# Lightning attention and a gated FFN on one core: q ahead of k in the block loads, a wait ahead of block 0's stores, four iotas in place of two and two adds

## The chip, the cores and the metric

The kernel runs on one core of a Trainium2 chip. A core has five engines with their own instruction queues: TensorE (PE in the profile, and PEld for its weight loads), VectorE (DVE), ScalarE (ACT), GpSimd (POOL) and SyncE (SP, which here only issues transfers). They meet through semaphores. Transfers are carried out by 16 DMA engines that all queues share. The metric is the device time of one execution in microseconds (us). Before the change it is 227.37 us, the median of 8 runs between 227.23 and 227.91.

## What is computed

Inputs are q, k, v of shape (4 batches, 8 heads, 768 positions, 64), one decay factor per head, and three FFN weight matrices (512 x 1536 twice, 1536 x 512). The first half is causal linear attention with decay, defined over blocks of 64 positions with a running state per batch and head; the second half is a feed-forward layer with a sigmoid gate on the 3072 tokens.

```
for b in range(nb):                       # blocks of 64 positions
    intra = einsum(qb, kb) * Dmask        # Dmask[i, j] = lam ** (i - j) for i >= j, else 0
    intra = einsum(intra, vb)
    inter = einsum(qb * lam_pow, kv_state)
    out[block] = intra + inter
    kv_state = lam ** 64 * kv_state + einsum(kb * rev_pow, vb)
...
gate = 1 / (1 + exp(-(x @ w_gate)))
out = (gate * (x @ w_val)) @ w_out        # fp32, 3072 x 512
```

## The kernel before

The 768 positions are cut into six steps n = 0 to 5 of 128 positions (the text calls them blocks 0 to 5), each with all four batches: 512 tokens. For every block PE does three things: the attention of the block; the two products with w_gate and w_val (`gp` and `vp` in `piece_gv`, L488), in 12 slices `ft` of 128 columns; and the product with w_out (`po`, L522), one per batch. While PE does the FFN of block n, the pieces of the attention of block n+1 are put between its slices. The order of every engine's instructions is the order in which the program emits them; no scheduler changes it. The list `more[ft]` in the main loop holds the pieces that are emitted after slice ft.

For a block from 2 on, the attention of that block uses these steps, named by function:

- `load` (L94 and L100): three transfers per q or k and one for v, issued on GpSimd's queue, from fp32 in HBM to bf16 in SBUF, in pieces of 64 numbers.
- `xbar` (L298): SyncE issues two transposing transfers, `kt<-kb` and `qt<-qb`, from SBUF to SBUF.
- `gate` (L615): GpSimd copies one column of each transposed tile to a scratch tile. Since GpSimd works in order, what it issues afterwards, v of the same block and k and q of the next, starts only when both transposes have landed. `next_loads(n)` emits `xbar(n)`, `gate(n)`, the load of v of n, and the loads of n+1.
- `e_q` (L277): VectorE multiplies the transposed q by a table of powers, giving QS, one instruction for two batches.
- `chunk_s` (L387, `sp`): PE multiplies QS with the transposed k, `kt`. `chunk_m` (L397): VectorE masks it.
- `piece_kd` (L127): ScalarE scales k, in four pieces of two heads, giving `kd`.
- `chunk_c` (L447, `cp`): PE multiplies `kd` with v, which yields the update of the state. `decayed` (L456, `xd`) is the old state times its decay on VectorE; `update_0` (L464) and `update_1` (L472) add the two.

In the loop for n = 1, which works ahead for block 2, `next_loads(2)` is emitted after slice 2, and right behind it, after slice 3, the eight stores of block 0's result, of 128 KB each. All of them are issued by SyncE, so its queue reads: the two transposes of block 2, eight stores of block 0, the two transposes of block 3 (emitted after slice 8), four stores of block 1, and so on. At the start of the program GpSimd issues the first loads between small table instructions; two of these are iotas that write a column each of `jn` (L174), the exponents of a block of 128, and two VectorE instructions in `chunk_rows` (L218, L219) turn them into exponents for half blocks of 64. `jn` is read by ScalarE in `tables_late`.

The lines in the main loop that set the places before the change are these:

```
more[2 + late + bp].append(do(e_q, nx, [2 * bp, 2 * bp + 1]))
more[4 + late].append(do(chunk_s, nx, bp))
more[8].append(do(chunk_c, nx, bp, cs))
more[6 + late].append(do(decayed, nx))
more[3 + late + i].append(kd(nx, 2 * i))
more[2].append(lambda: next_loads(2))
```

Here `nx` is n + 1 and `late` is 1 for n = 1 and 0 otherwise.

Of the kernel before, what the change touches and what calls it, by code (L numbers as in the profile page):

```python
# [16 lines left out]
def kernel(  # L17
# [11 lines left out]
    nc = tc.nc  # L29

    B, H, S, D = q.shape
    C = 128
# [28 lines left out]
    L = C // 2  # L61
    SYNC = mybir.DependencyInfo(mybir.DependencyClass.Sync, mybir.DependencyReason.DATA)
# [19 lines left out]
    def rows_of(u):  # L82
        return slice(u * 64, (u + 1) * 64)

    def load(n, what, b0=0, b1=B):
        sl = slice(n * C, (n + 1) * C)
        for c in what:
            if (c, n) not in T_:
                T_[c, n] = qkv.tile([128, B, H, D], BF16, tag=c + "b", name=c + "b",
                                      bufs=5 if c == "v" else 4)  # L90
            src = {"q": q, "k": k, "v": v}[c]
            nat = b1 if n == 0 or c == "v" else min(b1, NB2)
            if b0 < nat:
                nc.gpsimd.dma_start(  # L94
                    out=T_[c, n][:, b0:nat],
                    in_=src[b0:nat, :, sl, :].rearrange("b h s d -> s (b h) d"))
            if nat < b1:
                m = max(nat, b0)
                for u in range(2):
                    nc.gpsimd.dma_start(  # L100
                        out=T_[c, n][:, m:b1, u::2, :],
                        in_=src[m:b1, 1 - u::2, sl, :].rearrange("b h s d -> s (b h) d"))
# [29 lines left out]
    jn = const.tile([128, 2], FP32, tag="jn")  # L132
# [31 lines left out]
    for u in range(2):  # L164
# [4 lines left out]
                            pattern=[[1, C]], channel_multiplier=-1)  # L169
    nc.gpsimd.iota(ip1, pattern=[[1, C]], base=1, channel_multiplier=0,  # L170
                   allow_small_or_imprecise_dtypes=True)
    load(0, "k", 2, 4)
    for i, base in enumerate((-1, C - 1)):
        nc.gpsimd.iota(jn[:, i:i + 1], pattern=[[0, 1]], base=base, channel_multiplier=-1,  # L174
                       allow_small_or_imprecise_dtypes=True)
    nc.gpsimd.affine_select(out=tri, in_=tri, compare_op=ALU.is_gt, fill=1.0, base=0,
                            pattern=[[-1, C]], channel_multiplier=1)
# [35 lines left out]

    def powers(u):
        nc.scalar.activation(mask0[:, u], mask0[:, u], AF.Exp)

    def chunk_rows():
        nc.vector.tensor_scalar_add(jn[rows_of(1), 0:1], jn[rows_of(1), 0:1], float(L))  # L218
        nc.vector.tensor_scalar_add(jn[rows_of(0), 1:2], jn[rows_of(0), 1:2], -float(L))  # L219

    def tables_late():
        nc.scalar.activation(pk[:, 1], lnl, AF.Exp, scale=jn[:, 0:1])
# [37 lines left out]
    QT, KT = {}, {}  # L260
    tqs, tks = {}, {}

    def t_(c, n, bs, pool=ps_at, tag="ps"):
        ps = pool.tile([128, len(bs), HP, C], BF16, name="t" + c, tag=tag)
        for i, b in enumerate(bs):
            for hp in range(HP):
                nc.tensor.transpose(ps[:, i, hp, :], T_[c, n][:, b, 2 * hp:2 * hp + 2, :], ident)
        (tqs if c == "q" else tks)[n, bs[0]] = ps
# [24 lines left out]
        nc.vector.tensor_copy(T_[c, 0][:, b], H32[c, b])  # L293

    def xbar(n):
        for c, d in (("k", KT), ("q", QT)):
            d[n] = qtp.tile([128, B, HP, C], BF16, tag=c + "t", name=c + "t")
            nc.sync.dma_start_transpose(  # L298
                out=d[n].rearrange("p b hp s -> p (b hp) s"),
                in_=T_[c, n].rearrange("p b h d -> p (b h d)"))  # L300
        for b in range(B):
            KS[n, b] = KT[n][:, b]
# [172 lines left out]

    HT = {}

    def piece_gv(n, ft):  # L480
        fs = slice(ft * 128, (ft + 1) * 128)
        gp, vp = (ps_ff.tile([128, 2, TCH // 2], FP32, name=c, tag="ff") for c in ("gp", "vp"))
        sg = htp.tile([128, TCH], BF16, tag="sg", name="sg", bufs=3)
        whole, first, second = slice(0, 2), slice(0, 1), slice(1, 2)

        def product(ps, W, part):
            for mt in range(NMT):
                nc.tensor.matmul(ps[:, part], lhsT=W[:, mt, fs], rhs=XT[n][:, part, mt],  # L488
                                 start=(part is not second and mt == 0),
                                 stop=(part is not first and mt == NMT - 1), skip_group_check=True)  # L490

        order = [(gp, WG, whole), (vp, WV, whole)]
        if ft == 0 and n == 0:
            order = [(gp, WG, first), (gp, WG, second), (vp, WV, whole)]
        elif ft == 0 and n == 1:
            order = [(gp, WG, first), (vp, WV, first), (gp, WG, second), (vp, WV, second)]
        for ps, W, part in order:
            product(ps, W, part)
            if ps is gp and part is not first:
                nc.scalar.activation(sg, gp.rearrange("p a b -> p (a b)"), AF.Sigmoid)  # L500
        HT[n, ft] = htp.tile([128, TCH], BF16, tag="ht", name="ht", bufs=2 * NFT)
        if n < FIRST_XBAR:
            nc.vector.tensor_mul(HT[n, ft], sg, vp.rearrange("p a b -> p (a b)"))  # L503
        else:
            nc.vector.tensor_mul(HT[n, ft].rearrange("p (b c i) -> p c b i", b=B, c=2),  # L505
                                 sg.rearrange("p (c b i) -> p c b i", c=2, b=B),
                                 vp.rearrange("p c (b i) -> p c b i", b=B))

    OB, PO = {}, {}

    def store(n, tt, c0=0, c1=DM):
        (nc.scalar if (n, tt, c1) == (NSTEP - 1, B - 1, DM) else nc.sync).dma_start(out=out[tt * S + n * C:tt * S + (n + 1) * C, c0:c1],
                          in_=OB[n, tt][:, c0:c1])

    def piece_po(n, tt, c0, c1, eng, fts):
# [5 lines left out]
        for ft in fts:  # L521
            nc.tensor.matmul(po[:, :c1 - c0], lhsT=HT[n, ft][:, tt * 128:(tt + 1) * 128],  # L522
                             rhs=WO[:, ft, c0:c1], start=(ft == 0), stop=(ft == NFT - 1))
# [21 lines left out]
    cast_hw("k", 1)  # L545
    zeros(3)
    powers(1)
    chunk_rows()
    t_("q", 0, [0])
    e_q(0, [0], nc.vector)  # L550
    t_("q", 0, [1])
# [54 lines left out]
    load(1, "q", 2, 4)  # L606
    load(1, "v", 0, 2)
    load(1, "v", 2, 4)
    load(2, "kq")

    gates = const.tile([128, 2], BF16, tag="gates")

    def gate(n):
        for i, t in enumerate((KT[n], QT[n])):
            nc.gpsimd.tensor_copy(gates[:, i:i + 1], t[:, B - 1, HP - 1, C - 1:C])  # L615

    def next_loads(n):
        xbar(n)
        gate(n)
        load(n, "v")  # L620
        if n + 1 < NSTEP:
            load(n + 1, "kq")

# [5 lines left out]
    def gv(n, ft, *more):  # L631
        unit(lambda: piece_gv(n, ft), *more)

    def po(n, tt, *more, c=(0, DM), eng=nc.scalar, fts=range(NFT)):
        unit(lambda: piece_po(n, tt, *c, eng, fts), *more)
# [16 lines left out]
    def do(f, *args, **kw):  # L652
        return lambda: f(*args, **kw)
# [24 lines left out]
    def kd(n, h0, h1=None, **kw):  # L678
        return do(piece_kd, n, range(h0, h1 or h0 + 2), **kw)
# [20 lines left out]
    for n in range(1, NSTEP):  # L700
        nx = n + 1
        more = [[] for i in range(NFT)]
        if nx < NSTEP:
            late = 1 if n == 1 else 0
            cs = (0, 1) if nx < NSTEP - 1 else (0,)
            for bp in range(2):
                more[2 + late + bp].append(do(e_q, nx, [2 * bp, 2 * bp + 1]))
                more[4 + late].append(do(chunk_s, nx, bp))
                more[8].append(do(chunk_c, nx, bp, cs))
            for bp in range(2):  # L710
                more[4 + late + bp].append(do(chunk_m, nx, bp))
                more[8].append(do(update_0, nx, bp))
                if 1 in cs:
                    more[9 + bp].append(do(update_1, nx, bp))
            more[6 + late].append(do(decayed, nx))
            more[3 + late].insert(0, do(make_kd, nx))
            for i in range(4):
                more[3 + late + i].append(kd(nx, 2 * i))
            more[11].append(att(nx))
        if n == 1:  # L720
            more[0].append(chunk_lamq)
            more[2].append(lambda: next_loads(2))
            more[3].extend([lambda tt=tt, j=j: store(0, tt, 256 * j, 256 * j + 256)
                            for tt in range(B) for j in range(2)])
            more[8].append(lambda: next_loads(3))
        for ft in range(NFT):
            gv(n, ft, *more[ft])
        for tt in range(B):
            if n == NSTEP - 1 and tt == B - 1:
                po(n, tt, c=(0, 384), eng=nc.vector)  # L730
                po(n, tt, c=(384, 512))
            else:
                more = [lambda n=n: next_loads(n + 3)] if tt == B - 1 and n + 3 < NSTEP else []
                po(n, tt, *more)
# [35 lines left out]
```

## Time and profile before

| what | us |
|---|---|
| median of 8 runs | 227.37 |
| the profiled execution, its own time | 227.33 |
| its span in the profile | 225.5 |
| PE busy | 217.4 |
| DVE busy | 104.2 |
| ACT busy | 106.4 |
| POOL busy | 63.9 |
| share of the 16 DMA engines taken by GpSimd's queue (q0) | 86.9% |
| share taken by the hardware queue of SP (q1) | 20.1% |

The profile is of one execution whose time is inside the range of the runs. Its times count from the start of the span, and 1.8 us of the measured time lie around the span. PE is the busiest engine by far. A busy share is a mean over the whole span; where PE is idle, it must be read from the waits and from the order of time. The clock granted to PE is 1.00 throughout.

In the timeline, a line has the start, the length, engine and line, operation, what is written and read, and in square brackets the idle time before and what ended it. In the lists of transfers, the last number is the median time from issue to landing.

### The profile page before, as it was taken

Reading aid. Unit: us, or ns where it says so; the run is one execution under the profiler, and the core shown is the slowest. Engines: PE = TensorE matmul, PEld = TensorE weight load, DVE = VectorE, ACT = ScalarE, POOL = GpSimd, SP = SyncE. Lnnn points to the kernel's source line nnn. Section 1 sums busy time; section 2 is a strip of 40 time slices with the busy share of each in tenths; the row PEclk is TensorE's granted clock in tenths of the full one; section 3 lists DMA queues with packets and bytes.
Section 4 is the critical chain, followed back from the end, with each engine's and each line's share of the span. In section 5 each row is a group of like instructions: output and inputs, shape, how many; then the busy total and the mean of one; then the engine's idle time right before and its main releaser. Section 6 shows DMA issues by size and latency. Waiting matters only on the chain.

```text
span 225.5 us, 5209 instructions
## 1 busy us (share of the span) xinstructions
PE 217.4 (96%) x2187; PEld 106.1 (47%) x2187; DVE 104.2 (46%) x196; ACT 106.4 (47%) x232; POOL 63.9 (28%) x83
## 2 busy tenths in 40 slices
PE   7799999999997999999999999999999999999994
PEld 2454444557443544444544444544444444444443
DVE  4785553439478700478800378800378500333300
ACT  5777534494374342385342385342385342333221
POOL 7998865660085008401920030000000000000000
PEclk9999999999999999999999999999999999999999
DMA  7999999999989998997999839012100012100022
GB/s 112 151 160 184 196 202 179 172 154 141 175 201 159 141 199 104 207 167 140 85 156 185 181 60 89 3 49 93 47 3 0 0 51 94 47 0 0 4 93 94
DMA packets 106008, 25.25 MB, mean 112 GB/s; under 512 B 97152, under 2 KB 103552, under 8 KB 105984
## 3 DMA queue, kind: packets, MB, share of 16 engines
q0 software_dynamic: 82944, 13.90, 86.9%
q1 hardware_dynamic: 22752, 10.95, 20.1%
q8 instruction: 17, 0.28, 0.5%
q10 hardware_dynamic: 288, 0.07, 0.1%
q14 instruction: 7, 0.06, 0.1%
HBM read 28.32 MB, written 6.29 MB: 153 GB/s over the span
## 4 chain that ended last, share of the span: by engine, by line
PE 67%; DMA 23%; POOL 6%; issue 1%; SPq 1%; ACT 0%; POOLq 0%
PE po L522 23%; PE gp L488 20%; PE vp L488 20%; DMA WO<-in_moe_w_out_dram 6%; DMA kb<-in_k_dram 4%; DMA vb<-in_v_dram 4%; DMA WV<-in_moe_w_val_dram 4%; DMA WG<-in_moe_w_gate_dram 3%; DMA qt<-qb 2%; SPq L298 1%; POOL vb L94 1%; PE cp L447 1%; PE op L411 1%; PE op L425 1%; POOL WG L105 1%
## 5 line engine op out<-in xcount | busy, mean ns | idle before, releaser
L488 PE MATMUL gp<-XT,WG 128*128 128x512 bf16 (+1 forms) x296 | 74.2, 374 | 0.4 <-DMA WG<-in_moe_w_gate_dram 0.4
L488 PE MATMUL vp<-XT,WV 128*128 128x512 bf16 (+1 forms) x292 | 74.1, 376 | 0.0
L500 ACT ACTIVATE sg<-gp 128x512 bf16<-128x512 f32 x72 | 43.0, 597 | 64.8 <-PE gp L488 61.5
L505 DVE TENSOR_TENSOR ht<-sg,vp 128x512 bf16<-128x512 bf16 x48 | 33.0, 687 | 79.9 <-PE vp L488 79.9
L522 PE MATMUL po<-WO,ht 128*128 128x512 bf16 (+2 forms) x300 | 63.9, 371 | 0.0
L488 PEld LDWEIGHTS <-WV 128*128 128x128 bf16 x292 | 28.6, 98 | 33.4
L488 PEld LDWEIGHTS <-WG 128*128 128x128 bf16 x296 | 28.1, 98 | 32.3 <-DMA WG<-in_moe_w_gate_dram 1.1
L522 PEld LDWEIGHTS <-ht 128*128 128x128 bf16 x300 | 28.3, 98 | 31.9
L526 ACT COPY ob<-po 128x512 f32<-128x512 f32 (+1 forms) x24 | 13.7, 572 | 38.8 <-PE po L522 38.8
L127 ACT ACTIVATE kd<-kb,kds 128x128 bf16<-128x128 bf16 (+1 forms) x88 | 28.8, 400 | 0.0
L503 DVE TENSOR_TENSOR ht<-sg,vp 128x512 bf16<-128x512 bf16 x24 | 16.5, 686 | 13.2 <-PE vp L488 13.2
L615 POOL COPY gates<-kt 128x1 bf16<-128x1 bf16 x4 | 0.8, 188 | 50.6 <-DMA kt<-kb 50.6
L94 POOL DMA_DIRECT2D vb<-in_v_dram x9 | 11.9, 1334 | 2.5 <-issue 1.2
L318 DVE TENSOR_TENSOR MT<-sp,mask 128x512 bf16<-128x512 f32 x16 | 9.9, 683 | 2.9 <-PE sp L310 2.9
L437 ACT CAST XT<-op 128x512 bf16<-128x512 f32 x16 | 8.2, 599 | 5.0 <-PE op L425 5.0
L397 DVE TENSOR_TENSOR MT<-sp,mask 128x512 bf16<-128x512 f32 x16 | 10.3, 682 | 0.0
L100 POOL DMA_DIRECT2D qb<-in_q_dram x10 | 8.9, 907 | 2.5 <-DMA WO<-in_moe_w_out_dram 2.5
L100 POOL DMA_DIRECT2D kb<-in_k_dram x10 | 8.8, 893 | 2.0 <-DMA WO<-in_moe_w_out_dram 0.7
L94 POOL DMA_DIRECT2D qb<-in_q_dram x8 | 9.0, 1124 | 1.1 <-POOLq L754 0.8
L536 PE MATMUL zps<-st 128*128 128x512 bf16 x18 | 7.2, 544 | 1.5 <-DVE st L159 1.5
L94 POOL DMA_DIRECT2D kb<-in_k_dram x6 | 6.9, 1158 | 1.3 <-DMA WO<-in_moe_w_out_dram 0.8
L108 POOL DMA_DIRECT2D WV<-in_moe_w_val_dram x9 | 6.8, 764 | 1.2 <-DMA WG<-in_moe_w_gate_dram 0.8
(81 smaller groups left out, 114.6 us busy)
## 6 DMA issues: line engine op xcount, KB each, us to landing
out_dram<-ob SPq DMA_DIRECT2D x19, 256.0 KB, 2.1
vb<-in_v_dram POOLq DMA_DIRECT2D x4, 512.0 KB, 7.7
qb<-in_q_dram POOLq DMA_DIRECT2D x6, 256.0 KB, 9.9
kb<-in_k_dram POOLq DMA_DIRECT2D x6, 256.0 KB, 8.6
qb<-in_q_dram POOLq DMA_DIRECT2D x12, 128.0 KB, 9.3
WO<-in_moe_w_out_dram POOLq DMA_DIRECT2D x4, 384.0 KB, 12.2
kb<-in_k_dram POOLq DMA_DIRECT2D x10, 128.0 KB, 9.1
WG<-in_moe_w_gate_dram POOLq DMA_DIRECT2D x4, 256.0 KB, 7.5
```

The source lines that it names most:

```text
L94: nc.gpsimd.dma_start(out=T_[c, n][:, b0:nat], in_=src[b0:nat, :, sl, :].rearrange("b h s d -> s (b h) d"))
L100: nc.gpsimd.dma_start(out=T_[c, n][:, m:b1, u::2, :], in_=src[m:b1, 1 - u::2, sl, :].rearrange("b h s d -> s (b h) d"))
L127: nc.scalar.mul(KD[n][:, at, i, :], T_["k", n][:, at, i, :], kds[:, min(n // FIRST_XBAR, 1), h:h + 1])
L318: nc.vector.tensor_tensor(out=MT[n, b][:, u], in0=SP[n, b][u], in1=mask0[:, 1 - u if swapped(n, b) else u], op=ALU.mult)
L397: nc.vector.tensor_tensor(out=MT[n, bp][:, u], in0=SP[n, bp][u], in1=mask[:, u ^ bp].unsqueeze(1).to_broadcast([128, 2, HP, L]), op=ALU.mult)
L437: nc.scalar.copy(XT[n][:, c, :, bp * C:(bp + 1) * C], OP[n, c, bp].rearrange("p h j i -> p h (j i)"))
L488: nc.tensor.matmul(ps[:, part], lhsT=W[:, mt, fs], rhs=XT[n][:, part, mt], start=(part is not second and mt == 0), stop=(part is not first ...
L500: nc.scalar.activation(sg, gp.rearrange("p a b -> p (a b)"), AF.Sigmoid)
L503: nc.vector.tensor_mul(HT[n, ft], sg, vp.rearrange("p a b -> p (a b)"))
L505: nc.vector.tensor_mul(HT[n, ft].rearrange("p (b c i) -> p c b i", b=B, c=2), sg.rearrange("p (c b i) -> p c b i", c=2, b=B), vp.rearrange ...
L522: nc.tensor.matmul(po[:, :c1 - c0], lhsT=HT[n, ft][:, tt * 128:(tt + 1) * 128], rhs=WO[:, ft, c0:c1], start=(ft == 0), stop=(ft == NFT - 1))
L526: (eng.copy if eng is nc.scalar else eng.tensor_copy)(o, po[:, :c1 - c0])
```

## The change

The change has five edits.

1. For blocks 2 to 5, q is loaded and transposed ahead of k: the order is turned in `load(…, "qk")`, in `xbar` and in `gate`.
2. In the loop for n = 1 the eight stores of block 0 move from behind slice 3 to behind slice 7, and ahead of them SyncE gets an empty instruction that waits for the VectorE product of slice 7 of block 1 (`MUL[1, 7]`, the `ht` of that slice). SyncE's queue keeps its order: transposes of block 2, stores of block 0, transposes of block 3.
3. `decayed` moves from behind slice 6 (7 for n = 1) to behind slice 0 (2 for n = 1).
4. `make_kd` and the four `kd` pieces move from behind slices 3 to 6 to behind slices 4 to 7 for n = 2, 3, 4; for n = 1 they were there.
5. The two iotas over a full column of `jn` become four over half columns of 64 rows that write the half-block exponents directly, and `chunk_rows` with its two VectorE instructions goes.

PE's instructions and their order are the same as before.

```diff
     load(0, "k", 2, 4)
-    for i, base in enumerate((-1, C - 1)):
-        nc.gpsimd.iota(jn[:, i:i + 1], pattern=[[0, 1]], base=base, channel_multiplier=-1,
+    for u, i, base in ((0, 0, -1), (1, 0, -1), (0, 1, L - 1), (1, 1, L - 1)):
+        nc.gpsimd.iota(jn[rows_of(u), i:i + 1], pattern=[[0, 1]], base=base, channel_multiplier=-1,
                        allow_small_or_imprecise_dtypes=True)
...
-    def chunk_rows():
-        nc.vector.tensor_scalar_add(jn[rows_of(1), 0:1], jn[rows_of(1), 0:1], float(L))
-        nc.vector.tensor_scalar_add(jn[rows_of(0), 1:2], jn[rows_of(0), 1:2], -float(L))
...
     def xbar(n):
-        for c, d in (("k", KT), ("q", QT)):
+        for c, d in (("q", QT), ("k", KT)):
...
-            nc.vector.tensor_mul(HT[n, ft], sg, vp.rearrange("p a b -> p (a b)"))
+            mul = nc.vector.tensor_mul(HT[n, ft], sg, vp.rearrange("p a b -> p (a b)"))
...
+        MUL[n, ft] = mul.ins.name
...
-    load(2, "kq")
+    load(2, "qk")
...
     def gate(n):
-        for i, t in enumerate((KT[n], QT[n])):
+        for i, t in enumerate((QT[n], KT[n])):
...
         if n + 1 < NSTEP:
-            load(n + 1, "kq")
+            load(n + 1, "qk")
...
+            more[2 * late].append(do(decayed, nx))
             for bp in range(2):
...
-            more[6 + late].append(do(decayed, nx))
-            more[3 + late].insert(0, do(make_kd, nx))
+            more[4].insert(0, do(make_kd, nx))
             for i in range(4):
-                more[3 + late + i].append(kd(nx, 2 * i))
+                more[4 + i].append(kd(nx, 2 * i))
...
             more[2].append(lambda: next_loads(2))
-            more[3].extend([lambda tt=tt, j=j: store(0, tt, 256 * j, 256 * j + 256)
+            more[7].append(lambda: tc.add_manual_dep(nc.sync.nop().ins, MUL[1, 7], SYNC,
+                                                     reason="the loads ahead of the stores"))
+            more[7].extend([lambda tt=tt, j=j: store(0, tt, 256 * j, 256 * j + 256)
                             for tt in range(B) for j in range(2)])
```

More of the change, by code (lines that the diff above doesn't have):

```diff
@@ L474, in update_1 @@
                 in1=CP[n, bp][1][:, hp], op0=ALU.mult, op1=ALU.add)
-    HT = {}
+    HT, MUL = {}, {}
     def piece_gv(n, ft):
@@ L502, in piece_gv @@
         if n < FIRST_XBAR:
-            nc.vector.tensor_mul(HT[n, ft], sg, vp.rearrange("p a b -> p (a b)"))
+            mul = nc.vector.tensor_mul(HT[n, ft], sg, vp.rearrange("p a b -> p (a b)"))
         else:
-            nc.vector.tensor_mul(HT[n, ft].rearrange("p (b c i) -> p c b i", b=B, c=2),
+            mul = nc.vector.tensor_mul(HT[n, ft].rearrange("p (b c i) -> p c b i", b=B, c=2),
                                  sg.rearrange("p (c b i) -> p c b i", c=2, b=B),
                                  vp.rearrange("p c (b i) -> p c b i", b=B))
+        MUL[n, ft] = mul.ins.name
     OB, PO = {}, {}
@@ L547 @@
     powers(1)
-    chunk_rows()
     t_("q", 0, [0])
```

## The prediction, made before the changed kernel ran

> **What bounds the kernel now.** I read the page first: busy shares and the slices of the span.
>
> ```profile
> PE 217.4 (96%) x2187; PEld 106.1 (47%) x2187; DVE 104.2 (46%) x196; ACT 106.4 (47%) x232; POOL 63.9 (28%) x83
> PE   7799999999997999999999999999999999999994
> DMA  7999999999989998997999839012100012100022
> ```
>
> PE is the bound except in the first slices and in the thirteenth (a slice is 5.6 us), near 70 us. As the change leaves PE's work and order alone, all it can move is PE's idle time. Next, PE's waits, and PE's timeline for the attention of block 2 and, behind the first line of dots, the same steps of block 3.
>
> ```profile
> PE cp L447 <- DMA vb<-in_v_dram: 1.2, 1, 1.2
> PE sp L387 <- DVE QS L277: 0.4, 1, 0.4
> PE gp L488 <- DMA WG<-in_moe_w_gate_dram: 0.4, 2, 0.2
> ```
>
> ```profile
> 63.95 0.44 PE L387 MATMUL sp<-QS,kt 64*64 64x64 bf16 x32
> 64.84 0.45 PE L387 MATMUL sp<-QS,kt 64*64 64x64 bf16 x32 [0.45 <-DVE QS L277]
> 65.22 1.04 PE L488 MATMUL gp<-XT,WG 128*128 128x512 bf16 x4
> ...
> 71.82 0.73 PE L447 MATMUL cp<-vb,kd 64*64 64x64 bf16 x64 [1.25 <-DMA vb<-in_v_dram]
> ...
> 98.11 0.74 PE L387 MATMUL sp<-QS,kt 64*64 64x64 bf16 x64
> 98.78 1.04 PE L488 MATMUL gp<-XT,WG 128*128 128x512 bf16 x4
> ...
> 105.79 0.73 PE L447 MATMUL cp<-vb,kd 64*64 64x64 bf16 x64
> ```
>
> Undisturbed, sp takes 98.78 - 98.11 = 0.67 us; in block 2 it takes 65.22 - 63.95 = 1.27. That is 0.60 lost, because QS was late. From there to cp block 3 has four slices, 105.79 - 98.78 = 7.01, block 2 three; a slice is 1.73 (100.52 to 102.25), so cp could start at 65.22 + 7.01 - 1.73 = 70.50. It starts at 71.82: 1.32 lost to v. Together 1.92 us, the most that the change can give there. Behind it PE is saturated to the end, so what is gained at cp arrives in full.
>
> Then, why QS and v are late: the queues of SyncE and GpSimd, and the chain of waits.
>
> ```profile
> 54.67 3.21 SPq L298 DMA_TRANSPOSE kt<-kb  x1
> 57.98 2.96 SPq L298 DMA_TRANSPOSE qt<-qb  x1
> 61.00 4.01 SPq L512 DMA_DIRECT2D out_dram<-ob  x8
> 76.34 3.11 SPq L298 DMA_TRANSPOSE kt<-kb  x1
> ```
>
> ```profile
> 62.85 0.19 POOL L615 COPY gates<-qt 128x1 bf16<-128x1 bf16 x1 [1.81 <-DMA qt<-qb]
> 63.30 1.68 POOL L94 DMA_DIRECT2D vb<-in_v_dram  x1 [0.26 <-issue]
> ```
>
> ```profile
> 57.98 4.82 DMA qt<-qb
> 63.30 8.48 DMA vb<-in_v_dram
> ```
>
> v is issued only when the second transpose has landed, and takes 8.48 us to 71.78, with eight stores (1 MB) issued from 61.0 to 65.0. The lists of transfers give v's landing time in the stretches 60 to 80, 84 to 96, 106 to 118 and 131 to 145 (blocks 2 to 5):
>
> ```profile
> vb<-in_v_dram POOLq DMA_DIRECT2D x1, 512.0 KB, 8.5
> ...
> vb<-in_v_dram POOLq DMA_DIRECT2D x1, 512.0 KB, 8.0
> ...
> vb<-in_v_dram POOLq DMA_DIRECT2D x1, 512.0 KB, 7.4
> ...
> vb<-in_v_dram POOLq DMA_DIRECT2D x1, 512.0 KB, 6.9
> ```
>
> Blocks 2 and 3 have stores about them (block 1's four are issued from 82.86 to 90.5), blocks 4 and 5 none; block 5 has no further loads behind it either. What is slow is the start: the software queue moved 1013 packets from 63 to 68, 4.7 us after the issue, in block 2, but 1557 from 106 to 111, 4.2 us after the issue (106.80), in block 4. At the later full rate of 1235 per us (111 to 112) block 2 is (1557 + 0.5 x 1235 - 1013) / 1235 = 0.94 us behind.
>
> **The change part by part.** The sum starts from the profiled execution, 227.33 us with a span of 225.5; the median of the runs is 227.37, 0.04 more, which I neglect. About 0.2%, 0.45 us, can be told from no change.
>
> **q ahead of k.** Of block 2, three q loads pass three k loads on GpSimd's queue, the transposes swap on SyncE, the two gate copies (0.19 each) swap: nothing is added. As the loads have one shape, qt's transpose starts at 54.67 and lands as kt did, by 60.85; both QS (0.69 each) are then made behind slices 3 and 4 before PE arrives at 63.95. sp waits for kt instead, the second transpose, landed by 62.85: 1.1 to spare. So sp loses nothing, PE gains 0.60 and could start cp at 69.90. This alone is worth nothing in the end: v, at 71.78, would take it back.
>
> **The stores behind a wait.** The product of slice 7 ends at 69.03 + 0.68 = 69.71, and 0.60 earlier after the change: stores are issued from about 69.1 to 73.1 (4.01 for eight). Between the transposes and 70 us nothing but v, then q and k of block 3, is then on the DMA engines. First, the transposes. From the first issue to the second gate copy block 2 takes 62.85 - 54.67 = 8.18, block 4, without stores, 106.14 - 98.12 = 8.02, block 3 8.46. I take 8.02: the copy starts at 62.69, v is issued 0.45 later as before, at 63.14. Second, v itself: from 6.9 to 8.5. I take 7.4, that of block 4, which has the same q and k loads behind it and no stores. Third, the released stores may meet v's end. First store bytes come about 1 us after issue (issue 61.00; 251 packets of over 512 B from 62 to 63), so at 70.1, with v due at 70.54. Bounds: 0, and 2.3, since the one store that met loads took 4.2 instead of the median 1.9; a gain is excluded, as it is added traffic. I take 0.1, near the lower end, since four-tenths of a microsecond of overlap is left. v lands at 63.14 + 7.4 + 0.1 = 70.64; cp starts 0.04 later (71.78 to 71.82), at 70.68. PE gains 71.82 - 70.68 = 1.14. Late next is still v: PE, ready at 69.90, waits 0.78.
>
> Two rules of the Trainium skill differ from these rows. The packet counts of the software queue are 24 from 65 to 66 and 361 from 66 to 67, beside 149 and 4 of the hardware queue: when v's packets flow, the stores are nearly over. "DMA: Bandwidth & Descriptors", section "Queues, rings and completion order", says that each DMA engine takes turns between the queues for which it has packets; by that, stores could have cost v only the half microsecond in which both flowed, and the sum would be 227.33 - 0.16 - 0.5 = 226.7, an estimate, against 226.2 by the landing times. The same page, "Anatomy of one DMA — SWDGE (gpsimd) path", fits 2.0 us plus bytes over 436 GB/s, for v's 1.05 MB read 4.4 us; by that v would never be waited for and the sum is 225.4, but 6.9 is the least that any row of v here shows from block 2 on.
>
> **Behind the wait on SyncE's queue** stand the stores, block 3's transposes and block 1's stores. The stores are through the queue at 73.1, before block 3's transposes could go (76.34). Their 1 MB now shares with q and k of block 3: at 250 GB/s (their rate from 62 to 65) at most 4 us. Cover: block 3's second gate copy was at 84.80 and its sp at 98.11; GpSimd issues v of block 3 at 85.46, cp is at 105.79. Output buffers are reused by the copies of block 1's results, whose stores are issued from 82.86; block 0's would land by 79 even at 5.7 each (the slowest store row). Price 0.
>
> **decayed** (1.22 us on VectorE) goes, for block 2, behind the product of slice 2, where 1.04 is idle before the next; that one slips by some 0.1, and PE reuses its buffer a slice later. Nothing waited for xd before. 0; without cover 0.2.
>
> **kd a slice later** in blocks 3 to 5. In block 3 the last piece goes from 102.08 to 103.8 and ends at 105.06, cp is at 105.79: 0.73 to spare. 0; without cover at most a piece, 1.26, per block. The excluded gain: nothing waits for ScalarE there.
>
> **Iotas.** Two took 0.17 from start to start of what follows (4.72 to 4.89); two more add 0.17. Bounds: 0 (half a column, half the cost) and 0.6 (twice the 128x128 select, 0.30). I take 0.17 on GpSimd, 0 on the path: a 128 KB q piece issued in 0.95 lands 5.6 us later, the queue moves 2367 and 2380 packets in 6 to 8 and 8 to 10, 96% of 1235 per us, and at 20.01 GpSimd ends a wait of 0.77 for a landing. Without this cover the waits for WG at 15.89 and 19.76 (0.20 and 0.23) grow by 0.17 to 0.6, most of it absorbed in the new wait for v. VectorE's two instructions (0.15 each, 7.33 to 7.66) are followed by 0.92 of idle time: 0.
>
> **Sum:** 227.33 - 1.14 = 226.2.
>
> **The rivals.** *The stores are not what makes v slow.* Its first packet comes 2.2 us after the issue in blocks 2 and 4 alike. Then v takes 8.48 from 63.14, cp starts at 71.66: 227.2. Against it stand four blocks in the right order. *v comes in time.* With block 5's 6.9, cp starts at 70.08: 225.6; landed by 69.86, all 1.92: 225.4. Against it: other loads follow this v. *Slower: the released stores run into v.* If v still starts as slowly as before, 3395 of its 4096 packets are through at 70.0, and the stores come at 70.1 among the last 700. The mechanism decides once the end of v stretches by 0.6 (0.16 gained plus 0.45); at the 2.3 above the time is 229.5, at 0.6 227.8. *That the wait does nothing*: unlikely, as the first store waits on VectorE's count.
>
> **How the numbers follow.** My forecast, v taking 7.0 to 8.0: 0.68, with 225.8 to 226.8. v in time 0.14, stores innocent 0.11, slower 0.06, else 0.01. Range 225.5 (v at 6.9, a little sooner) to 227.2 (stores innocent); outside stay the slower case and half of the full gain. Faster 0.83, same 0.10, slower 0.07.
>
> **What would show it.** No wait of sp for QS; stores from 69 us; v's landing time near 7.4 for block 2, more packets in the first 5 us; a wait of cp of 0.5 to 1.0 us. Wrong if v takes 8.5 without stores, if cp waits for kd in blocks 3 to 5, or if waits for WG grow past 0.3.

## The result, and the profile after

The changed kernel takes 225.96 us, the median of 13 runs between 225.69 and 226.93, beside 227.4 us of the kernel before (36 runs). The ratio is 0.9941 with a 95% interval from 0.9927 to 0.9955: 1.0 to 1.7 us faster. The profiled execution took 225.69 us with a span of 223.9, beside 227.33 and 225.5: 1.6 us less. The runs of the changed kernel, here and in two later sets, lie in two groups, 18 up to 226.17 and 8 from 226.46 on; the three profiled ones are of the first, so the waits read from them are those of the quicker group.

The page of the changed kernel, busy shares and slices:

```profile
PE 216.8 (97%) x2187; PEld 106.0 (47%) x2187; DVE 103.9 (46%) x194; ACT 106.4 (47%) x232; POOL 64.8 (29%) x85
PE   7798999999999999999999999999999999999994
DMA  7999999999969999999499959012100012100022
```

The dent in PE's row near 70 us is gone. One in the fourth slice is new. All waits of PE that the profile lists for it:

```profile
PE zps L533 <- DVE st L159: 1.5, 1, 1.5
PE tq L263 <- DMA qb<-in_q_dram: 0.9, 1, 0.9
PE gp L484 <- DMA WG<-in_moe_w_gate_dram: 0.8, 2, 0.7
PE sp L306 <- ACT KS L284: 0.5, 1, 0.5
PE tk L263 <- POOL jn L174: 0.2, 1, 0.2
```

The waits of sp for QS and of cp for v have left the list; the wait for WG has grown from 0.4 to 0.8. PE's timeline in block 2's attention:

```profile
64.23 0.74 PE L383 MATMUL sp<-QS,kt 64*64 64x64 bf16 x64
64.89 1.04 PE L484 MATMUL gp<-XT,WG 128*128 128x512 bf16 x4
...
70.23 0.73 PE L443 MATMUL cp<-vb,kd 64*64 64x64 bf16 x64
```

sp takes 64.89 - 64.23 = 0.66 instead of 1.27, and cp starts at 70.23 instead of 71.82 without a wait. PE arrived at sp 0.28 later than before (63.95), because of the longer wait for WG at the start: the 1.92 lost before, less 0.28, is the 1.6 us of the span.

The queues of SyncE and GpSimd, and the transfer of v:

```profile
54.47 3.26 SPq L294 DMA_TRANSPOSE qt<-qb  x1
57.84 3.09 SPq L294 DMA_TRANSPOSE kt<-kb  x1
69.46 5.37 SPq L509 DMA_DIRECT2D out_dram<-ob  x8
75.46 5.14 SPq L294 DMA_TRANSPOSE qt<-qb  x1
82.22 3.04 SPq L294 DMA_TRANSPOSE kt<-kb  x1
```

```profile
4.72 0.99 POOL L174 IOTA jn<- 64x1 f32 x4
5.79 0.30 POOL L176 TENSOR_SCALAR_AFFINE_SELECT tri<-tri 128x128 f32<-128x128 f32 x1
...
62.57 0.19 POOL L611 COPY gates<-kt 128x1 bf16<-128x1 bf16 x1 [1.36 <-DMA kt<-kb]
63.02 1.68 POOL L94 DMA_DIRECT2D vb<-in_v_dram  x1 [0.26 <-issue]
```

```profile
vb<-in_v_dram POOLq DMA_DIRECT2D x1, 512.0 KB, 7.2
```

The stores are issued from 69.46 on, but their queue (q1) has no packet from 72 to 73 and its first 95 from 73 to 74. v is issued at 63.02 and lands 7.2 us later, at 70.2, which is where cp starts: v and PE arrive together in this execution, and v is in before the first store packet flows. v's start is quicker, as the prediction named for a sign: from 63 to 68 the software queue (q0) starts 2560 packets, where it started 1013. The iotas and what they hold up cost GpSimd 5.79 - 4.72 = 1.07 instead of 0.17.

### The profile page after: what moved, and what is told of

It reads as the page before. It is cut to its first block, busy times and chain, and to the rows that moved or that the text cites. A ratio compares the mean times of both kernels' runs of the same rounds, so it can differ in the third digit from the quotient of the medians.

```text
span 223.9 us, 5209 instructions
## 1 busy us (share of the span) xinstructions
PE 216.8 (97%) x2187; PEld 106.0 (47%) x2187; DVE 103.9 (46%) x194; ACT 106.4 (47%) x232; POOL 64.8 (29%) x85
## 4 chain that ended last, share of the span: by engine, by line
PE 91%; POOL 4%; DMA 3%; issue 1%; ACT 0%; POOLq 0%
PE po L519 28%; PE gp L484 28%; PE vp L484 27%; DMA WG<-in_moe_w_gate_dram 3%; POOL vb L94 1%; PE sp L383 1%; PE cp L443 1%; PE op L407 1%; PE op L421 1%; POOL qb L94 1%; PE cp L359 1%; PE sp L306 0%; PE op L337 0%; PE tq L263 0%; PE tk L263 0%
## 5 line engine op out<-in xcount | busy, mean ns | idle before, releaser
L611 POOL COPY gates<-qt 128x1 bf16<-128x1 bf16 x4 | 1.1, 272 | 49.6 <-DMA qt<-qb 49.6
```

## The experiments

Three questions were open after the result: which of the edits carries the gain, what makes v slow, and whether the iotas, whose cost on GpSimd was far above the forecast, cost the kernel anything. Each set of four kernels ran on one chip beside runs of the kernel before; ratios are to those. v's landing times and waits are those of one profiled execution of each kernel in each set.

**q ahead of k alone**

```diff
 (kernel before)
-        for c, d in (("k", KT), ("q", QT)):
+        for c, d in (("q", QT), ("k", KT)):
...
-    load(2, "kq")
+    load(2, "qk")
...
-        for i, t in enumerate((KT[n], QT[n])):
+        for i, t in enumerate((QT[n], KT[n])):
...
-            load(n + 1, "kq")
+            load(n + 1, "qk")
```

> The kernel before with q ahead of k alone. Theory (v is the last wait in block 2, and the stores set when it lands): sp no longer waits for QS and loses nothing, but v lands as late as before, some 8.5 us after its issue; PE waits for it 0.60 us longer at cp, about 1.85 instead of 1.25, and the time stays at 227.2 to 227.5. Rival (the 0.60 us at sp is a gain of its own): 226.8, cp 0.5 us sooner.

Measured: ratio 1.0054 (1.0028 to 1.0080), slower. sp lost nothing and v took it back, as expected, and more: v took 9.1 us instead of some 8.5, and cp waited 2.46 instead of 1.85. The rest was not expected. Its timeline of PE, and then stretches of 1 us with the granted clock in the third column from the end:

```profile
72.40 0.73 PE L447 MATMUL cp<-vb,kd 64*64 64x64 bf16 x64 [2.46 <-DMA vb<-in_v_dram]
73.07 1.29 PE L488 MATMUL gp<-XT,WG 128*128 128x512 bf16 x4
74.15 1.91 PE L488 MATMUL vp<-XT,WV 128*128 128x512 bf16 x4
```

```profile
73.00:74.00 1.00, 1.00 (x19) 0.48 (x6) 1.00 (x2) 0.00 (x0) 0.00 (x0) 0.85 2.43 151
74.00:75.00 1.00, 1.00 (x3) 0.30 (x2) 0.18 (x1) 0.60 (x1) 0.00 (x0) 0.50 2.44 155
75.00:76.00 1.00, 1.00 (x4) 0.44 (x3) 0.00 (x0) 0.00 (x0) 0.00 (x0) 0.50 2.48 156
76.00:77.00 1.00, 1.00 (x4) 0.32 (x3) 0.82 (x2) 0.00 (x0) 0.00 (x0) 0.50 2.50 154
77.00:78.00 1.00, 1.00 (x5) 0.39 (x4) 0.90 (x4) 0.45 (x1) 0.00 (x0) 0.94 1.94 118
```

About a microsecond after PE went on, its clock was granted at half for some 3.4 us: two products took 1.91 and 1.66 instead of 1.03. Of the six runs, two took 227.8, with a mean clock of 1.00, as the kernel before beside them (227.72); four took 229.3 to 229.7, with a mean clock of 0.983 to 0.992. So the reorder alone is worth nothing where the clock holds, and the runs with a lower clock take 1.5 to 1.9 us more.

**The wait ahead of the stores alone**

```diff
 (kernel before; k stays ahead of q)
-            more[3].extend([lambda tt=tt, j=j: store(0, tt, 256 * j, 256 * j + 256)
+            more[7].append(lambda: tc.add_manual_dep(nc.sync.nop().ins, MUL[1, 7], SYNC,
+                                                     reason="the loads ahead of the stores"))
+            more[7].extend([lambda tt=tt, j=j: store(0, tt, 256 * j, 256 * j + 256)
```

> The kernel before with the wait ahead of block 0's stores alone, k still ahead of q. Theory (the stores slow v's start): QS is still made around v's issue, at 62.9 and 64.1, sp still loses 0.60; v lands 7.2 to 7.4 us after its issue, at about 70.4, so cp starts at 70.5 without a wait or nearly so; 226.0. Rival (v starts slowly because VectorE multiplies QS while GpSimd writes v's descriptors, and the change only moved QS away from there): v takes 8.3 to 8.5 us, 227.3.

Measured: 0.9966 (0.9954 to 0.9979), 0.8 us faster than the 227.72 beside it. The waits of PE in block 2:

```profile
PE cp L447 <- DMA vb<-in_v_dram: 0.8, 1, 0.8
PE sp L387 <- DVE QS L277: 0.3, 1, 0.3
```

Both waits are left, shortened, a part of it because PE reached sp 0.20 later in this execution (64.15). v took 8.0: better than 8.5, not the 7.2 to 7.4 expected. QS was made as before, around v's issue, and still v gained, so the stores matter; why v did not come down to 7.4 this run does not tell.

**The changed kernel with the old iotas**

```diff
 (changed kernel)
-    for u, i, base in ((0, 0, -1), (1, 0, -1), (0, 1, L - 1), (1, 1, L - 1)):
-        nc.gpsimd.iota(jn[rows_of(u), i:i + 1], pattern=[[0, 1]], base=base, channel_multiplier=-1,
+    for i, base in enumerate((-1, C - 1)):
+        nc.gpsimd.iota(jn[:, i:i + 1], pattern=[[0, 1]], base=base, channel_multiplier=-1,
...
+    chunk_rows()
     t_("q", 0, [0])
```

> The changed kernel with the two full-column iotas and the two VectorE instructions of before. Theory (the four half-column iotas hold GpSimd up by 0.9 us, and of that 0.29 reaches PE as longer waits for WG and nothing later takes it back): waits for WG 0.4 instead of 0.8 in all, everything from 20 us on 0.25 to 0.3 sooner, 225.4 to 225.7 beside 225.9 of the changed kernel. Rival (what PE wins at the start it loses again waiting for v, since v is issued by the DMA engines' pace and not by PE's): cp waits 0.2 to 0.3 for v and the time is 225.9.

Measured: 0.9962 (0.9950 to 0.9975). Both theories were wrong. The waits for WG did fall to 0.2, and PE reached sp at 63.88, 0.35 sooner than in the changed kernel. But cp waited 1.28 us, since v took 7.9, issued at 63.24. The iotas are not a cost that can be taken out; with the old ones v is later. Beside the hold alone (226.91), this kernel (226.86) has q ahead of k and the moved pieces in addition, and they gain nothing that these runs can tell.

**The stores back in their old place**

```diff
 (changed kernel)
-            more[7].append(lambda: tc.add_manual_dep(nc.sync.nop().ins, MUL[1, 7], SYNC,
-                                                     reason="the loads ahead of the stores"))
-            more[7].extend([lambda tt=tt, j=j: store(0, tt, 256 * j, 256 * j + 256)
+            more[3].extend([lambda tt=tt, j=j: store(0, tt, 256 * j, 256 * j + 256)
```

> The changed kernel with block 0's stores back behind slice 3 and no wait, all else kept. Theory: the stores run from 61 to 66, v takes 8.3 to 8.5 us from its issue at about 63.1 and lands at 71.5; cp waits about 1.2 us; 227.1 to 227.4, the gain gone. Rival (moving QS ahead of v's issue is what made v faster): v takes 7.2 and the time stays at 225.9.

Measured: 0.9978 (0.9965 to 0.9991). v was issued at 63.54, took 8.0 and cp waited 1.72. Of the changed kernel's gain, 0.46% to 0.59% in its three sets, 0.22% is left without the wait: half to two thirds of it is gone. The rival, that moving QS brings v down to 7.2, falls, as QS is early here too. This kernel shows no wait for WG at all, with the new iotas: the 0.28 us lost at the start of the changed kernel's profiled execution is not a fixed price of the iotas.

**The changed kernel again, and the four iotas alone**

```diff
 (changed kernel, unaltered)
```

> The changed kernel once more, unaltered, beside the runs of this set, since the same kernels came out 0.3 us apart from one set of runs to the next. Theory 1 (v's landing time differs between executions by up to 0.8 us even with the stores held): v 7.2 to 8.0, ratio to before 0.994 to 0.996. Theory 2 (the two full-column iotas of the third kernel made v late): v 7.2 and a ratio of 0.994 again.

```diff
 (kernel before)
-    for i, base in enumerate((-1, C - 1)):
-        nc.gpsimd.iota(jn[:, i:i + 1], pattern=[[0, 1]], base=base, channel_multiplier=-1,
+    for u, i, base in ((0, 0, -1), (1, 0, -1), (0, 1, L - 1), (1, 1, L - 1)):
+        nc.gpsimd.iota(jn[rows_of(u), i:i + 1], pattern=[[0, 1]], base=base, channel_multiplier=-1,
...
-    chunk_rows()
```

> The kernel before with the four half-column iotas alone. GpSimd reaches the next select 0.9 us later. Theory 1 (the q loads and weights behind it are held up by the pace of the DMA engines; the 0.29 us that PE was late in the changed kernel was chance or is absorbed by the wait for v): waits for WG between 0 and 0.8, time within 0.4 us of before, 227.0 to 227.6. Theory 2 (0.29 us reach PE and the end): 227.7. Slower still, 229 and more, if the wait for v passes 2 us and the clock falls.

Measured: the changed kernel 0.9954 (0.9936 to 0.9971), v 7.2 from 63.13, cp waiting 0.52, no wait for WG, as the second theory has it. The iotas alone 0.9993 (0.9982 to 1.0004), no change: v took 8.1, 0.4 less than before, but was issued at 63.88, and sp still waited 0.53 for QS.

**decayed and kd left where they were**

```diff
 (changed kernel)
-            more[2 * late].append(do(decayed, nx))
...
-            more[4].insert(0, do(make_kd, nx))
+            more[6 + late].append(do(decayed, nx))
+            more[3 + late].insert(0, do(make_kd, nx))
             for i in range(4):
-                more[4 + i].append(kd(nx, 2 * i))
+                more[3 + late + i].append(kd(nx, 2 * i))
```

> The changed kernel with decayed and the kd pieces left where they were. Theory: the two moves cost and gain nothing; no wait of PE for kd or for VectorE in either, the same time as the changed kernel run beside it within 0.3 us. Rival (xd behind slice 7 delays the product of slice 8 and with it PE, so the move is part of the gain): 0.2 to 0.6 us slower than the changed kernel.

Measured: 0.9955 (0.9939 to 0.9971) beside 0.9954. The two moves are worth nothing that these runs can tell, and no wait of PE for kd, or for VectorE behind the start of the program, stands in either list. In this profile and in that of the iotas alone the first transpose of block 2 started at 55.16 and 55.18, some 0.6 later than in the others (54.3 to 54.7); why, the runs do not tell. This profiled execution, 226.42, lies between the two groups of the changed kernel's runs; whether such late transposes make the upper group is open.

**The stores held one slice longer**

```diff
 (changed kernel)
-            more[7].append(lambda: tc.add_manual_dep(nc.sync.nop().ins, MUL[1, 7], SYNC,
+            more[8].append(lambda: tc.add_manual_dep(nc.sync.nop().ins, MUL[1, 8], SYNC,
                                                      reason="the loads ahead of the stores"))
-            more[7].extend([lambda tt=tt, j=j: store(0, tt, 256 * j, 256 * j + 256)
+            more[8].extend([lambda tt=tt, j=j: store(0, tt, 256 * j, 256 * j + 256)
```

> The changed kernel with the stores of block 0 held one slice longer, behind the product of slice 8, still ahead of block 3's transposes: they start at 70.5 to 71 instead of 69.1 to 69.8. Theory 1 (the released stores meet the end of v and stretch it from 7.2 to 7.9): v lands 7.2 us after its issue every time, cp waits 0 to 0.6, up to 0.7 us faster than the changed kernel beside it where that one has v at 7.9. Theory 2 (the end of v is not touched by the stores): the same time as the changed kernel, v 7.2 to 8.0 alike.

Measured: 0.9948 (0.9932 to 0.9965), not to be told from the 0.9954 beside it. Stores from 70.64, v 7.3, cp waiting 0.56. The released stores do not stretch v's end, and the packets tell why: v has landed at 70.3, and q1 has no packet before 74 here and none before 73 in the changed kernel's first profile. Holding the stores from 69 on is enough.

**Old iotas beside the changed kernel itself**

After this, v with the stores held had taken 7.1 to 7.3 in four profiles with the new iotas and 7.9 to 8.0 in two with the old, but those with the old came from another chip than three of the four. A third set put both on one chip.

```diff
 (changed kernel, unaltered)
```

> The changed kernel, unaltered, as the measure for the other three of this set. v of block 2 7.1 to 8.0 us from its issue, cp waits 0 to 1.3, ratio to before 0.993 to 0.997.

```diff
 (changed kernel, with the two iotas and chunk_rows as above)
```

> The changed kernel with the two full-column iotas of before, a second time, now beside the changed kernel itself. Theory (v's landing differs from chip to chip; the iotas have nothing to do with it): the same v landing as the changed kernel beside it within 0.3 us, and the same time within 0.3 us. Rival (with the old iotas v takes 7.9 instead of 7.2): 0.5 to 0.7 us slower than the changed kernel beside it.

Measured: the changed kernel 0.9949 (0.9931 to 0.9967), median 225.91; with the old iotas 0.9968 (0.9954 to 0.9982), median 226.49. v took 7.1 and 7.8, issued at 62.93 and 63.20. The theory of the chip falls; the rival holds in the profiles, while the two intervals of the time, each against the kernel before, still overlap.

What can two instructions at 5 us do to a transfer at 63 us? The profile lists small transfers of kind "instruction", 8 KB each, on queue 14. The queues of the two kernels of this set from 63 to 65, and then from 65 to 70:

The changed kernel:

```profile
q14 instruction: 1, 0.01, 1.0%
...
q0 software_dynamic: 5234, 0.67, 208.9%
```

With the old iotas (nothing of q14 from 63 to 65):

```profile
q0 software_dynamic: 4824, 0.62, 192.5%
q14 instruction: 1, 0.01, 0.4%
```

In the changed kernel that packet goes before v's own packets flow, with the old iotas in the midst of them. The packets of all twelve profiles of the study in which v is loaded behind the gate sort the same way:

| stores of block 0 | q14 packet after v's issue, us | v's landing, us |
|---|---|---|
| at 61, k or q first, old iotas | 4.2, 5.4 | 8.5, 9.1 |
| at 61, new iotas | 1.0, 1.0 | 8.0, 8.1 |
| held, old iotas | 3.8, 3.6, 3.6 | 8.0, 7.9, 7.8 |
| held, new iotas | 1.0, 1.0, 1.2, 1.3, 1.0 | 7.2, 7.2, 7.1, 7.1, 7.3 |

By the means of the rows, the wait ahead of the stores takes 0.9 off v's time with either iotas, the iotas' edit 0.7 with the stores in either place. The two act on different parts of the transfer. In the 6.2 us after v's issue q0 starts 4065 to 4201 packets with the stores held and the new iotas, and 3832 to 4088 with the old, which is 0.15 us apart on average at the full rate of 1235 per us, while the landings are 0.7 apart; with the stores at 61 it starts 2176 to 3274, about 1 us behind. So the stores delay the flow as a whole, and the iotas' edit the last of v's packets.

That the edit moves the q14 packet is shown. That the packet, 0.3 to 0.4 us long in most of these profiles, is what holds v's end up is inferred from its place: it would have to hold up one of the 16 engines with its part of v, the profile does not tell which engine carries a packet, and the 0.7 is longer than the packet itself.

**v ahead of the gate**

```diff
 (changed kernel)
     load(2, "qk")
+    load(2, "v")
...
-        load(n, "v")
+        if n != 2:
+            load(n, "v")
```

> The changed kernel with v of block 2 loaded right behind its q and k, ahead of the gate, so that it does not wait for the transposes. Theory (v's landing is the only wait left in block 2, and it is late because it is issued behind the gate): v lands near 61, cp never waits, all of the 1.92 us lost before in block 2 is back; 225.3 to 225.6, the runs closer together than the changed kernel's. Rival (v's packets now run beside the transposes and delay kt, which is then what sp waits for): sp waits for kt, 0.5 to 1.5 us, 226 or more.

```diff
 (the same, and in addition)
-            more[7].append(lambda: tc.add_manual_dep(nc.sync.nop().ins, MUL[1, 7], SYNC,
-                                                     reason="the loads ahead of the stores"))
-            more[7].extend([lambda tt=tt, j=j: store(0, tt, 256 * j, 256 * j + 256)
+            more[3].extend([lambda tt=tt, j=j: store(0, tt, 256 * j, 256 * j + 256)
```

> The kernel of the run before, but with block 0's stores back behind slice 3 without a wait. Theory (the wait ahead of the stores is worth something only because v is in flight there): the same time as with the wait, within 0.3 us. Rival (the stores also delay the transposes, so that sp waits for kt): 0.3 us or more slower, a wait of sp.

Measured: 1.0119 (1.0088 to 1.0149) and 1.0121 (1.0088 to 1.0155). The theory falls and its rival is right, harder than expected. Waits and transposes of the first of the two:

```profile
PE sp L383 <- DMA kt<-kb: 3.2, 1, 3.2
```

```profile
vb<-in_v_dram POOLq DMA_DIRECT2D x1, 512.0 KB, 15.5
...
qt<-qb SPq DMA_TRANSPOSE x1, 10.9
```

and the transposes of the changed kernel beside it:

```profile
qt<-qb SPq DMA_TRANSPOSE x1, 6.6
kt<-kb SPq DMA_TRANSPOSE x1, 4.8
```

With v's packets beside them, the transposes take 10.9 instead of 6.6, and 6.9 instead of 4.8 for kt, and sp waits 3.2 us for kt. The second kernel has the same wait; in its profiled execution the clock was granted at 0.50 from about 66.2, still within the wait, to 73. That the wait ahead of the stores makes no difference there agrees with the theory that its worth lies in v, but with sp this late it tells little. The gate in front of v pays for itself.

These two kernels also say something of the q14 packet. Against the changed kernel the first alters nothing but the place of v's load in GpSimd's order, and the packet, at 64.0 to 64.1 in the changed kernel, comes between 53 and 55 in both. It moves with GpSimd's instructions, to which the iotas' edit adds two; that they are what it brings is likely, but not shown.

No kernel of the study is shown to beat the changed one.

## Why the prediction was right, point by point

The forecast was 226.2 with 225.5 to 227.2; the measured 225.96 lies inside. Its course was the forecast one: QS and v were what block 2 lost, v is still the last wait, and what is gained at cp reaches the end. That the sum came so close is luck: two errors in v's landing, of 0.3 to 0.5 and of 0.7, go against each other.

- *The most that the change can give is 1.92 us, and behind cp PE is saturated.* Right: 1.92 less the 0.28 that PE came later is the 1.6 of the span.
- *q ahead of k gains 0.60 at sp, and alone is worth nothing.* Right, where the clock held (227.8 beside 227.72). That a longer wait can halve the clock was no part of the forecast; the reorder without the wait ahead of the stores is a loss. In the changed kernel it seems to be worth nothing either. No run leaves it alone out, but in three profiles with k ahead (before, hold alone, iotas alone) the second half of sp started 1.98 to 1.99 after the second gate copy, and from there the rows before give 0.38 + 5.28 to cp. With the second gate copy at 62.57, 62.68 and 62.48 in the three executions of the changed kernel, cp would have started at 70.22, 70.33 and 70.13 with k ahead, an estimate; it started at 70.23, 70.41 and 70.09.
- *v is issued at 63.14.* 63.02, 63.13 and 62.93 in three executions of the changed kernel. Right.
- *Without the stores v takes 7.4, and 0.1 for their release.* The mechanism was right and the size too large. With the stores held and nothing else of the start changed, v takes 7.8 to 8.0, not 7.5. Their release costs nothing: the prediction had their first bytes at 70.1, about 1 us after the issue as before the change, but in three executions they flow only from 72.7 to 73.5 on, when v has landed. This part of the sum was mis-sized by 0.3 to 0.5.
- *The iotas cost 0.17 on GpSimd and 0 on the path.* This is the step that failed. They cost 0.90 more on GpSimd than before, above the upper bound of 0.6: each takes 0.17 to 0.22 to the next and the last one 0.40, where the two full columns followed each other in under 0.1. And the edit is worth some 0.7 of v's landing, a gain for which the sum had no term. Beside the old iotas on the same chip the median differs by 0.58 us. That PE is 0.28 late at the start in one profile, and not at all in two others, was foreseen as what the new wait would absorb.
- *PE then waits 0.78 at cp.* 0.52 in two executions, nothing in the one where PE came late.
- *decayed and kd at 0.* Right: 0.9955 beside 0.9954.
- *Behind the wait on SyncE's queue: at most 4 us for block 3, under a cover of 13.* The price of 0 was right, the bound too low: v of block 3 is issued at 89.11, 90.46 and 89.98 in three executions instead of 85.46, so 3.65 to 5.0 later, and nothing in block 3 waits.
- *The rivals.* "The stores are not what makes v slow" falls: v takes 0.9 less with them held, with either iotas. (v's first packet comes 2.45 and 2.38 after the issue in blocks 2 and 4, not 2.2; they are alike all the same.) "v comes in time" is what the profiled execution shows, helped by PE's late start. "The released stores run into v" falls: they flow only after v has landed.

The rule of the Trainium skill that was weighed ("DMA: Bandwidth & Descriptors", "Queues, rings and completion order": engines take turns between queues that have packets) was given half a microsecond of common flow, and so 226.7. That half microsecond was a reading cut short: it ended at 67, and in the kernel before the stores have more packets from 67 to 68.

```profile
q0 software_dynamic: 628, 0.08, 124.7%
q1 hardware_dynamic: 134, 0.12, 46.2%
```

So the estimate of 226.7 does not test the rule. The runs show 0.9 us less for v with the stores held. How the stores slow v's start is open: in this microsecond both queues together take less of the engines' time, as the profile counts it, than v's queue alone takes later (124.7% and 46.2% beside 247.0% from 71 to 72), so a mere sharing of busy engines does not explain it. The page's fit of 4.4 us for v is as far off as forecast, with 7.1 to 9.1 in the profiles with v behind the gate; the measurement decides.

## What to carry to other kernels

Price a group of edits by the wait that ends last, and then test the edits one by one: here the one that looked like housekeeping took almost as much off that wait as the one with the hold, though alone, with the stores in the way, it gained nothing. An edit that removes a wait in front of another wait only lengthens the second, and here a wait of TensorE that grew to 2.46 us was followed by a fall of the clock that cost 1.5 to 1.9 us. Before a load is moved ahead of a gate, look at what its packets would run beside: v's 512 KB in small packets cost the first transpose 4 us.

## What the runs showed of the hardware that was not expected

- After an idle stretch of 2.46 us TensorE's clock was granted at 0.50 for about 3.4 us in the profiled run of the reorder alone, and four of its six runs show the loss; idle for 1.72 us in another profile, it stayed at 1.00; with 3.2 us it fell in one profile, for 6.8 us, and not in another. The Trainium skill, "TensorE: Matmul & The Clock Gate", section "Part 1: The HAM clock gate (the "warmup" mystery)", has a window of some 3.4 us that runs freely; that fits both the length of the slow stretch, once and twice, and that the same idle time does not always meet it. The page's table wants at least one idle window for the fall; 2.46 us is less than that, and the measurement decides.
- An 8 KB transfer of instructions falls into the window of a data transfer or not, as instructions come or go nearly 60 us earlier, and where it does, the data land 0.7 us later; that the one causes the other is inferred.
- Four iotas on 64 rows by one column take 1.07 us to the next instruction where two on 128 rows take 0.17. The last of the four alone is 0.40 long.
- With a load of 512 KB in packets of under 512 bytes in flight in addition, a DMA transpose took 10.9 us instead of 6.6, and the next 6.9 instead of 4.8.
- Stores issued while the software queue was busy had their first packets some 4 us after the issue (69.46, 73 to 74); before the change it was about 1 us (61.00, 62 to 63).
